# Attention output with queries on partitions from chunk 8 on, its transpose made by the DMA crossbar, and q loaded in token order

## The chip, the cores and the metric

One core of one Trainium2 chip. The metric is the time of one execution on the device, in microseconds (us), lower is better. Before: 225.88 us, median of 3 runs (223.73 to 227.31). Every later run stands beside runs of the kernel before on the same chip, since its medians differed between the chips used, from 224.75 to 226.15 us. Runs more than 1.5% above the fastest of the same kernel are marked slow and left out of the ratios.

## The reference, cut to what matters

```python
# q, k, v: [4 batches, 8 heads, 768 tokens, 64], float32; lam: one decay per head
# attention with exponential decay, block by block (64 tokens each in the reference)
intra = (qb @ kb.T) * Dmask          # Dmask[i, j] = lam ** (i - j) for j <= i, else 0
out   = intra @ vb + (qb * lam_pow) @ kv_state
kv_state = lam_block * kv_state + (kb * rev_pow).T @ vb
x = out.transpose(0, 2, 1, 3).reshape(3072, 512)
h = x @ w_in                          # [3072, 2048]
g = where(h >= 1, h, where(h <= -1, 0, (h + 1) ** 2 / 4))
return g @ w_out                      # [3072, 512], float32
```

## The kernel before

It works in 24 chunks of 128 tokens; four chunks make a stage of 512 tokens for the two dense layers. All loads of q, k and v, all crossbar transposes and all stores of the output are issued by SyncE (SP), one after the other. A scheduler in the kernel, run while it is built, decides the order on each engine: every operation is added with an engine, an estimate, its prerequisites and a due time.

The path of a chunk: load k, q, v in float32; GpSimd (POOL) scales k and q by powers of the decay into bf16 (`ks`, `qs`); SP issues the crossbar transposes of both (`kT`, `qT`, from chunk 6 on; before that TensorE transposes); TensorE forms scores (`ps`, `pt`); VectorE masks them (`sc`); TensorE forms the output (`po`), and ScalarE copies it as x^T (`xT`) into the operand of the first layer.

```python
def f_kx(c):                                   # one crossbar transpose of k for each chunk
    kT[c] = qtp.tile([128, HP, 128], BF16, name="kT", tag="kT")
    nc.sync.dma_start_transpose(out=kT[c], in_=ks[c].rearrange("p h d -> p (h d)"))

def f_qx(m, e):                                # and two of q for each pair of chunks
    nc.sync.dma_start_transpose(out=qT_tile(m)[:, e], in_=qs[m, e].rearrange("p h d -> p (h d)"))
# ...
def f_o(c):                                    # output: features on partitions, tokens as columns
    for hp in range(HP):
        if cb > 0:
            nc.tensor.matmul(po[:, hp], lhsT=ubd[(c - 1) % NUB][:, hp, :], rhs=q_cols(c, hp),
                             start=True, stop=False)
        for hi in range(2):                    # v is padded with zeros to 128 columns
            nc.tensor.matmul(po[:, hp], lhsT=vi[c % NV][:, hp, hi].rearrange("p a d -> p (a d)"),
                             rhs=sc_sb[c][:, hi, hp, :], start=(cb == 0 and hi == 0), stop=(hi == 1))
# ...
def f_load(c, x, wait):                        # q: a pair of chunks in one load, 512 B pieces
    if x == 0:
        t = lq.tile([128, H, 2, D], F32, name="x0f", tag="x0f")
        i = q[b, :, s0:s0 + 2 * C, :].rearrange("h (j e) d -> j h (e d)", e=2)
        d = nc.sync.dma_start(out=t.rearrange("p h e d -> p h (e d)"), in_=i)
```

## Time and profile before

| | before |
|---|---|
| median | 225.88 us |
| profiled run | span 224.4 us, clock 0.999, fast |
| TensorE busy | 206.8 us (92%) |
| from chunk 8's k load to the last q or k transpose | 51.2 to 155.0 us: 103.8 us, 87 issues on SP |

The last row is a count of mine: in the trace of SP, from the issue of the load of chunk 8's k to the issue of the last transpose of q or k. I call it the queue's stretch and use it for every kernel below. In the views, PE is TensorE, PEld its weight loads, DVE VectorE, ACT ScalarE, POOL GpSimd and SPq the issuing by SP; L362 is line 362 of that kernel's file; `ph`, `py` and `pu` hold results of the first layer, the second layer and the state.

The prediction shows the busy table and the slices. Two more views of the kernel before are needed to compare. The first is the chain of work that ended last, as shares of the span; the second is TensorE's one wait for the landing of a transfer (us in total, times, longest):

```profile
PE 62%; DMA 17%; SPq 5%; POOL 5%; issue 3%; ACT 3%; DVE 3%; POOLq 0%; ACTq 0%
```

```profile
PE ps L314 <- DMA kT<-ks: 0.6, 1, 0.6
```

TensorE waits 0.6 us for a transpose in the whole run. And this is what SP does (start us, length us, line, operation):

```profile
84.28 0.58 SPq L460 DMA_DIRECT2D x0f<-in_q_dram  x1
85.37 1.20 SPq L286 DMA_TRANSPOSE kT<-ks  x1
86.64 0.56 SPq L464 DMA_DIRECT2D x1f<-in_k_dram  x1
87.30 0.52 SPq L464 DMA_DIRECT2D x2f<-in_v_dram  x1
87.87 1.18 SPq L464 DMA_DIRECT2D x1f<-in_k_dram  x1
89.16 3.06 SPq L289 DMA_TRANSPOSE qT<-qs  x2
```

Add a start and its length, and the next start follows within 0.05 to 0.5 us. The lengths in the whole stretch sum to 98.1 of its 103.8 us: SP issues almost without a pause, though the prediction counted only 70 us of shortest issue times (0.58 us a load, 1.2 a transpose, 0.37 a store). So 28 us are issues that took longer than their shortest, as the 3.06 us for two transposes above; what SP spends them on, the profile doesn't show. In the transposes it is not waiting for data: counted chunk by chunk, each transpose of k or q in the stretch was issued 2.7 to 9.6 us after GpSimd had written its source. I had these rows before I predicted, and did not sum them.

### The profile page before, as it was taken

The page shows a single profiled execution, that of the slowest core. Times are in us where ns is not written, and L with a number is a line of the kernel's source. Part 1 is how long each engine was busy: PE and PEld are TensorE (multiplying, and loading weights), DVE is VectorE, ACT ScalarE, POOL GpSimd, SP SyncE. Part 2 cuts the span into 40 slices and gives each one's busy share as a digit, 9 for nine tenths or more (in the row PEclk, how much of TensorE's full clock was granted, in tenths as well). Part 3 has the DMA queues.
Part 4 walks back from the last instruction along what each step waited for, and adds up shares of the span by engine and source line. Part 5 has one row for each costly group of instructions (what it writes and reads, how often), then busy time and mean ns, then how long its engine had stood idle before and what let it go on. Part 6 is the DMA issues. An engine that isn't in the chain of part 4 may idle for free.

```text
span 224.4 us, 4691 instructions
## 1 busy us (share of the span) xinstructions
PE 206.8 (92%) x1904; PEld 136.4 (61%) x1904; DVE 144.0 (64%) x218; ACT 123.5 (55%) x221; POOL 64.8 (29%) x65
## 2 busy tenths in 40 slices
PE   0497997999998999999989999999999999999993
PEld 0385544768577877777666766677767744444442
DVE  2678198879949786779387439976656554554301
ACT  3455767547547676666467456676655445445120
POOL 7471084026716360916151028521000000000000
PEclk9999999999999999999999999999999999999999
DMA  5999999999799999989999899986111001110212
GB/s 132 244 192 201 196 243 199 175 208 243 106 232 196 188 207 192 168 211 126 221 151 316 220 197 252 232 159 152 47 47 50 15 31 50 47 47 0 93 50 95
DMA packets 89974, 34.40 MB, mean 153 GB/s; under 512 B 70368, under 2 KB 87008, under 8 KB 89952
## 3 DMA queue, kind: packets, MB, share of 16 engines
q1 hardware_dynamic: 85584, 29.89, 67.2%
q0 software_dynamic: 4224, 4.19, 11.9%
q8 instruction: 15, 0.25, 0.5%
q14 instruction: 7, 0.06, 0.1%
q10 hardware_dynamic: 144, 0.00, 0.0%
HBM read 27.27 MB, written 6.29 MB: 150 GB/s over the span
## 4 chain that ended last, share of the span: by engine, by line
PE 62%; DMA 17%; SPq 5%; POOL 5%; issue 3%; ACT 3%; DVE 3%; POOLq 0%; ACTq 0%
PE py L405 25%; PE ph L362 25%; DMA x0f<-in_q_dram 8%; DMA x2f<-in_v_dram 5%; DMA x1f<-in_k_dram 4%; PE po L334 3%; POOL ks L242 3%; SPq L286 3%; POOL qs L246 2%; PE ps L314 2%; SPq L464 1%; ACT r L370 1%; PE po L331 1%; PE pu L295 1%; PE py L399 1%
## 5 line engine op out<-in xcount | busy, mean ns | idle before, releaser
L362 PE MATMUL ph<-xT,w_in_sb 128*128 128x128 bf16 (+2 forms) x880 | 94.0, 255 | 1.4 <-ACT r L370 1.4
L370 ACT ACTIVATE r<-ph,one 128x512 bf16<-128x512 f32 (+2 forms) x96 | 64.6, 679 | 52.5 <-PE ph L362 34.2
L405 PE MATMUL py<-w_out_sb,gT 128*128 128x512 bf16 x368 | 92.1, 379 | 0.0
L362 PEld LDWEIGHTS <-w_in_sb 128*128 128x128 bf16 x880 | 65.4, 98 | 24.9 <-issue 2.8
L378 DVE TENSOR_SCALAR t<-r 128x1024 bf16<-128x1024 bf16 x48 | 27.3, 570 | 40.3 <-ACT r L370 40.3
L405 PEld LDWEIGHTS <-gT 128*128 128x128 bf16 x368 | 33.9, 98 | 31.4 <-DVE gT L386 0.2
L386 DVE TENSOR_TENSOR gT<-w,t 128x1024 bf16<-128x1024 bf16 x48 | 41.2, 858 | 1.7
L246 POOL TENSOR_TENSOR qs<-x0f,tab_q 128x512 bf16<-128x512 f32 x24 | 29.5, 1250 | 37.1 <-DMA x0f<-in_q_dram 21.9
L381 DVE TENSOR_TENSOR w<-r,t 128x1024 bf16<-128x1024 bf16 x48 | 37.3, 777 | 1.3
L242 POOL TENSOR_TENSOR ks<-x1f,tab_k 128x512 bf16<-128x512 f32 x20 | 25.4, 1275 | 37.4 <-DMA x1f<-in_k_dram 17.5
L324 DVE TENSOR_TENSOR sc<-ps,causal 128x512 bf16<-128x512 f32 x20 | 13.8, 690 | 13.6 <-PE pt L314 13.4
L410 ACT COPY osb<-py 128x512 f32<-128x512 f32 x23 | 13.5, 587 | 12.0 <-PE py L405 10.1
L341 ACT CAST xT<-po 128x512 bf16<-128x512 f32 x24 | 14.1, 587 | 10.7 <-PE po L334 5.5
L334 PE MATMUL po<-sc,vi 128*128 128x128 bf16 x192 | 18.9, 224 | 0.6 <-DVE sc L322 0.5
L260 ACT CAST vi<-x2f 128x512 bf16<-128x512 f32 x24 | 14.8, 618 | 7.8 <-DMA x2f<-in_v_dram 7.8
L299 ACT CAST ubd<-pu 64x256 bf16<-64x256 f32 x40 | 14.6, 365 | 5.2 <-PE pu L295 4.9
L334 PEld LDWEIGHTS <-vi 128*128 128x128 bf16 x192 | 15.0, 101 | 3.2 <-issue 1.3
L331 PE MATMUL po<-qT,ubd 128*128 128x128 bf16 x80 | 14.8, 221 | 0.2 <-ACT xT L341 0.2
L324 DVE TENSOR_TENSOR sc<-pt,causal 128x512 bf16<-128x512 f32 x20 | 13.6, 680 | 0.0
L265 PE MATMUL pt<-ident,ks 128*128 128x128 bf16 x24 | 2.8, 249 | 8.2 <-DVE ks L242 8.0
L331 PEld LDWEIGHTS <-ubd 128*128 128x128 bf16 x80 | 7.9, 99 | 1.6
L295 PE MATMUL pu<-vi,ks 128*128 128x128 bf16 x80 | 8.2, 228 | 0.3
(55 smaller groups left out, 88.2 us busy)
## 6 DMA issues: line engine op xcount, KB each, us to landing
x1f<-in_k_dram SPq DMA_DIRECT2D x24, 256.0 KB, 5.3
x0f<-in_q_dram SPq DMA_DIRECT2D x12, 512.0 KB, 5.5
x2f<-in_v_dram SPq DMA_DIRECT2D x24, 256.0 KB, 5.4
out_dram<-osb SPq DMA_DIRECT2D x23, 256.0 KB, 2.7
w_in_sb<-in_moe_w_in_dram POOLq DMA_DIRECT2D x4, 512.0 KB, 8.7
w_out_sb<-in_moe_w_out_dram POOLq DMA_DIRECT2D x4, 512.0 KB, 8.7
qT<-qs SPq DMA_TRANSPOSE x18, 4.4
kT<-ks SPq DMA_TRANSPOSE x18, 3.5
```

Of the source, the lines that this page charges most:

```text
L242: eng.tensor_tensor(ks[c], qkv_ld[c, 1], _bc(tab_k[:, c % NCB, :], 2, D), op=AX.mult)
L246: eng.tensor_tensor(qs[m, e], qkv_ld[m, 0][:, :, e], _bc(tab_q[:, e, m % (NCB // 2), :], 2, D), op=AX.mult)
L260: nc.scalar.copy(out=v_out(vi[c % NV]), in_=qkv_ld[c, 2].rearrange("p (a b) d -> p a b d", b=2))
L324: nc.vector.tensor_tensor(sc_sb[c][:, g], pst[c, g], _bc(causal, 1, HP), op=AX.mult)
L331: nc.tensor.matmul(po[:, hp], lhsT=ubd[(c - 1) % NUB][:, hp, :], rhs=q_cols(c, hp), start=True, stop=False)
L334: nc.tensor.matmul(po[:, hp], lhsT=vi[c % NV][:, hp, hi].rearrange("p a d -> p (a d)"), rhs=sc_sb[c][:, hi, hp, :], start=(cb == 0 and hi ...
L362: nc.tensor.matmul(ph[:, j * m:(j + 1) * m], lhsT=w_in_sb[:, ko, (ni + j) * 128:(ni + j + 1) * 128], rhs=xT[s][:, ko, part * m:(part + 1) ...
L370: nc.scalar.activation(out=r_t[grp][:, i, cs], in_=ph_t[s, ni, part][:, cs], func=AF.Relu, bias=one[:, 0:1])
L378: nc.vector.tensor_scalar(t_t[grp], r, 0.5, 1.0, op0=AX.mult, op1=AX.min)
L381: nc.vector.tensor_tensor(w_t[grp], r, t_t[grp], op=AX.subtract)
L386: nc.vector.tensor_tensor(gT[s][:, f - RW * n:f, part * m:(part + 1) * m], w_t[grp].rearrange("p a (b m) -> p (a b) m", m=m), t_t[grp].rea ...
L405: nc.tensor.matmul(py_t[s, ms], lhsT=gT[s][:, ko, ms * 128:(ms + 1) * 128], rhs=w_out_sb[:, ko, :], start=(ko == 0), stop=(ko == FO - 1))
```

## The change

The intent: half of the columns of v that the output's products load are zeros. With the masked scores as weights and v streaming, a head needs 64 columns in place of 128. The output then has queries on partitions, so x must be transposed before the first layer; that is one crossbar transpose for a chunk, off TensorE. Now q is the weight operand of the state's product; it is no longer read in the interleaved order of a pair of chunks but loaded in token order, one load for each chunk in 256 B pieces. The scheduler is told to want the outputs 6 us earlier. Chunks 0 to 7 stay as they are.

```diff
+    DX, DLEAD = 8, 6000
 def f_o(c):
+        if c >= DX:
+            for hp in range(HP if cb > 0 else 0):
+                nc.tensor.matmul(po[:, hp], lhsT=q_cols(c, hp), rhs=ubd[(c - 1) % NUB][:, hp, :],
+                                 start=(hp == 0), stop=True, skip_group_check=True)
+            for h in range(H):
+                nc.tensor.matmul(po[:, h // 2, HD[h % 2]], lhsT=sc_sb[c][:, h % 2, h // 2, :], rhs=vn[c][:, h, :],
+                                 start=(cb == 0 and h == 0), stop=True, skip_group_check=True)
+            return
 def f_x(c):
+        if c >= DX:
+            x_sb[c] = xsp.tile([128, d_model], BF16, name="xs", tag="xs")
+            nc.scalar.copy(out=x_sb[c], in_=pot[c].rearrange("p a b -> p (a b)"))
+            return
+    def f_xx(c):
+        nc.sync.dma_start_transpose(out=xT[sx][:, :, off:off + C], in_=x_sb[c])
 def f_load(c, x, wait):
+        if x == 0 and c >= DX:
+            if c % 2 == 0:
+                qkv_ld[c // 2, 0] = lq.tile([128, 2, H, D], F32, name="x0f", tag="x0f")
+            d = nc.sync.dma_start(out=qkv_ld[c // 2, 0][:, c % 2], in_=q[b, :, s0:s0 + C, :].rearrange("h p d -> p h d"))
-        od, cb = o_due(c), c % NCB
+        od, cb = o_due(c) - (DLEAD if c >= DX else 0), c % NCB
+        if c >= DX:
+            add(("x", c), "SP", 1200, lambda c=c: f_xx(c), [("xs", c)], due=-3, dma=640)
# ... cut: tables and mask for token order, contiguous copy of v, prerequisites, order of the first loads
```

More of the change, by code (lines that the diff above doesn't have):

```diff
@@ L76 @@
     xp = ctx.enter_context(tc.tile_pool(name="xp", bufs=3))
+    xsp = ctx.enter_context(tc.tile_pool(name="xsp", bufs=2))
+    vnp = ctx.enter_context(tc.tile_pool(name="vnp", bufs=4))
     gp = ctx.enter_context(tc.tile_pool(name="gp", bufs=2))
@@ L134, with late_setup @@
         nc.vector.memset(t, 0.0)
+    tab_qn = const.tile([128, NCB, H], F32)
+    causal_n = const.tile([128, 128], F32)
+    def late_setup():
+        nc.scalar.activation(out=tab_qn, in_=arg[:, 0], func=AF.Exp)
+        nc.gpsimd.memset(causal_n, 1.0)
+        nc.gpsimd.affine_select(out=causal_n, in_=causal_n, compare_op=AX.is_ge, fill=0.0,
+                                base=0, pattern=[[1, 128]], channel_multiplier=-1)
     def v_out(t):
@@ L245, in cast_q @@
         qs[m, e] = qkp.tile([128, H, D], BF16, name="qs", tag="qs")
+        if 2 * m >= DX:
+            eng.tensor_tensor(qs[m, e], qkv_ld[m, 0][:, e], _bc(tab_qn[:, (2 * m + e) % NCB, :], 2, D), op=AX.mult)
+            return
         eng.tensor_tensor(qs[m, e], qkv_ld[m, 0][:, :, e], _bc(tab_q[:, e, m % (NCB // 2), :], 2, D), op=AX.mult)
@@ L255, in q_cols @@
         i = c % 2
+        if c >= DX:
+            return qT[c // 2][rows, i, hp, :]
         x = qT[c // 2][rows, 0, hp, i * 64:(i + 1) * 64]
         return bass.AP(x.tensor, x.offset, [list(x.ap)[0], [HP * 128, 2], [1, 64]])
+    vn, x_sb = {}, {}
     def cast_v(c):
+        if c == CPS:
+            late_setup()
+        if c >= DX:
+            vn[c] = vnp.tile([128, H, D], BF16, name="vn", tag="vn")
+            nc.scalar.copy(out=vn[c], in_=qkv_ld[c, 2])
+            return
         nc.scalar.copy(out=v_out(vi[c % NV]), in_=qkv_ld[c, 2].rearrange("p (a b) d -> p a b d", b=2))
@@ L294, in f_u @@
         for hp in range(HP):
-            nc.tensor.matmul(pu[0][:, hp, :], lhsT=pair(ks[c], hp), rhs=v_pair(vi[c % NV], hp),
+            nc.tensor.matmul(pu[0][:, hp, :], lhsT=pair(ks[c], hp), rhs=v_pair(vi[c % NV], hp) if c < DX else pair(vn[c], hp),
                              start=(c % NCB == 0 and hp == 0), stop=True, skip_group_check=True)
@@ L323, in f_m @@
         else:
-            nc.vector.tensor_tensor(sc_sb[c][:, g], pst[c, g], _bc(causal, 1, HP), op=AX.mult)
+            nc.vector.tensor_tensor(sc_sb[c][:, g], pst[c, g], _bc(causal if c < DX else causal_n, 1, HP), op=AX.mult)
     def f_o(c):
@@ L328, in f_o @@
         po = pot[c] = pp_o.tile([128, HP, 128], F32, name="po", tag="po")
+        if c >= DX:
[5 more added lines that the diff above has]
+                                 start=(cb == 0 and h == 0), stop=True, skip_group_check=True)
+            return
         for hp in range(HP):
@@ L340, in f_x @@
             xT[sx] = xp.tile([128, KO, MS], BF16, name="xT", tag="xT")
+        if c >= DX:
+            x_sb[c] = xsp.tile([128, d_model], BF16, name="xs", tag="xs")
+            nc.scalar.copy(out=x_sb[c], in_=pot[c].rearrange("p a b -> p (a b)"))
+            return
         nc.scalar.copy(out=xT[sx][:, :, off:off + C].rearrange("p h (j e) -> p h j e", e=2),
                        in_=pot[c].rearrange("p h (e j) -> p h j e", e=2))
+    def f_xx(c):
+        sx, off = c // CPS, (c % CPS) * C
+        nc.sync.dma_start_transpose(out=xT[sx][:, :, off:off + C], in_=x_sb[c])
     gT, r_t, t_t, w_t, py_t, ph_t, osb = {}, {}, {}, {}, {}, {}, {}
@@ L456, in f_load @@
         b, s0 = c // NCB, (c % NCB) * C
-        if x == 0:
+        if x == 0 and c >= DX:
+            if c % 2 == 0:
+                qkv_ld[c // 2, 0] = lq.tile([128, 2, H, D], F32, name="x0f", tag="x0f")
+            d = nc.sync.dma_start(out=qkv_ld[c // 2, 0][:, c % 2], in_=q[b, :, s0:s0 + C, :].rearrange("h p d -> p h d"))
+        elif x == 0:
             t = lq.tile([128, H, 2, D], F32, name="x0f", tag="x0f")
@@ L482 @@
             need = [("w",) + w_seen[-1], ("cast", CPS - 1, 1) if len(w_seen) > 1 else None] if w_seen else \
-                [("cast", CPS - 2, 2), ("cast", CPS - 2, 1)]
+                [("cq", CPS // 2 - 1, 1)]
             if gated is not None:
@@ L493 @@
         gated = len(w_seen) - 2 if last_c is not None and w_seen and not isinstance(order[order.index(it) - 1], int) else None
-        for x in (1, 2) if it % 2 else (1, 0, 2) if it == 0 else (0, 1, 2):
+        for x in (1, 0, 2) if it == 0 or it >= DX else (1, 2) if it % 2 else (0, 1, 2):
             need = [("w",) + w_seen[-2] if w_seen else None]
-            if x == 0:
+            if x == 0 and it >= DX:
+                add(("ld", it, 0), "SP", 590, lambda i=it: f_load(i, 0, None),
+                    [("cq", it // 2 - LQ, 0), ("cq", it // 2 - LQ, 1)] + need, due=pos_ * 1e-3, dma=1190)
+            elif x == 0:
                 add(("lq", it // 2), "SP", 700, lambda i=it, wait=gated: f_load(i, 0, wait),
@@ L516 @@
             add(("cq", m, i), "POOL", 1060, lambda m=m, i=i: cast_q(m, i, nc.gpsimd),
-                [("lq", m), ("cq", m, 0) if i else None, old, ("qT",) + old[1:]])
+                [("lq", m) if c < DX else ("ld", c + i, 0), ("cq", m, 0) if i else None, old, ("qT",) + old[1:]])
             if m < XQ:
@@ L542 @@
             add(("s", c, 0), "PE", mm(*[128] * 4) + 190, lambda c=c: f_s2(c),
-                [("kT", c) if c < XT else ("t", c), ("qT", m, 0), ("qT", m, 1), ("m", c - 1, 0), ("m", c - 1, 1)], due=od - 2500, extra=FILL)
+                [("kT", c) if c < XT else ("t", c), ("qT", m, 0) if c < DX or c % 2 == 0 else None, ("qT", m, 1) if c < DX or c % 2 else None, ("m", c - 1, 0), ("m", c - 1, 1)], due=od - 2500, extra=FILL)
         for h in range(2):
@@ L548 @@
             add(("m", c, h), "DVE", 690, lambda c=c, h=h: f_m(c, h), [("s", c, h if c < CPS else 0), ("o", c - 3), ("m", c, 0) if h else None])
-        add(("o", c), "PE", mm(*[128] * (12 if cb else 8)), lambda c=c: f_o(c),
+        add(("o", c), "PE", mm(*[128] * (12 if cb else 8)) if c < DX else mm(*[128] * (4 if cb else 0)) + 8 * 33, lambda c=c: f_o(c),
             [("m", c, 1), ("cast", c, 2), ("ub", c - 1, 0) if cb else None, ("ub", c - 1, 1) if cb else None,
-             ("x", c - 1), ("o", c - 1)], due=od, extra=FILL)
-        add(("x", c), "ACT", 600, lambda c=c: f_x(c), [("o", c), ("x", c - 1), ("l1", (c // CPS - 2) * FO - 1)])
+             ("x", c - 1) if c <= DX else ("xs", c - 1), ("o", c - 1)], due=od, extra=FILL)
+        add(("x", c) if c < DX else ("xs", c), "ACT", 600, lambda c=c: f_x(c),
+            [("o", c), ("x", c - 1), ("xs", c - 1), ("x", c - 2), ("l1", (c // CPS - 2) * FO - 1)])
+        if c >= DX:
+            add(("x", c), "SP", 1200, lambda c=c: f_xx(c), [("xs", c)], due=-3, dma=640)
     n1, last = 0, None
```

## The prediction

> **What bounds the kernel now.** I read the busy table and the slices of the page first, then the groups of instructions, then the sums by stretch of time, the chain of waits, and last the order of TensorE and of the DMA queue instruction by instruction.
>
> ```profile
> PE 206.8 (92%) x1904; PEld 136.4 (61%) x1904; DVE 144.0 (64%) x218; ACT 123.5 (55%) x221; POOL 64.8 (29%) x65
> ...
> PE   0497997999998999999989999999999999999993
> ...
> DMA  5999999999799999989999899986111001110212
> ...
> q1 hardware_dynamic: 85584, 29.89, 67.2%
> ```
>
> TensorE is busy 92% and its empty slices are the first few and the last. "Busy" flatters a pipelined engine, so I laid the start times of successive matmuls against the spacing of an undisturbed stream (56 ns for 128 columns, 216 ns for 512). From 40 us to the end only some 6 us are lost, 2.3 us of them in three waits, at 69.7, 113.0 and 133.6 us; about 11 us are lost between 8 and 40 us, and the first matmul starts at 7.9 us. So from 40 us on a microsecond taken out of TensorE's stream comes off the end, if nothing else takes its place.
>
> The second row matters as much: the DMA engines are as full as TensorE until about 155 us, then nearly empty. All loads of q, k and v, all crossbar transposes and all stores are issued by one queue, SP. By stretch (start:end, length, busy time of PE, PEld, DVE, ACT, POOL, clock, DMA share, GB/s):
>
> ```profile
> 89.50:92.50 3.00, 3.00 (x37) 2.19 (x35) 2.93 (x4) 2.35 (x4) 2.90 (x3) 1.00 1.37 217
> ...
> 104.00:107.00 3.00, 3.00 (x46) 2.32 (x44) 2.96 (x5) 2.06 (x5) 0.75 (x1) 1.00 0.63 129
> ...
> 180.00:200.00 20.00, 20.00 (x94) 9.11 (x93) 10.87 (x18) 9.37 (x15) 0.00 (x0) 1.00 0.07 27
> 40.00:150.00 110.00, 108.18 (x1214) 78.15 (x1213) 82.78 (x115) 67.03 (x121) 44.18 (x35) 1.00 1.09 200
> ```
>
> The first is load traffic, the second a row of transposes alone, which leaves the engines half empty; from 40 to 150 us the mean share is 1.09 (two packets may be in flight on one engine), and after 180 us it is 0.07. The chain of waits between 60 and 113 us is not TensorE but a loop of SP, DMA and POOL:
>
> ```profile
> 66.73 1.19 SPq L286
> 67.97 3.64 DMA x1f<-in_k_dram
> 71.78 1.57 POOL ks L242
> 73.34 1.01 SPq L286
> 74.40 4.44 DMA x0f<-in_q_dram
> ```
>
> A load lands, POOL scales it, SP issues its transpose, and the next load stands behind it in the same queue. Here two paths run side by side, nearly equally long.
>
> **What the Trainium skill says.** "TensorE: Matmul & The Clock Gate", section Back-to-back issue gap, gives about 60 cycles for 1 to 64 columns against 134 for 128, with a floor near 25 ns, or near 62 ns if the sequencer decodes matmuls. The second floor cannot hold here: matmuls of 128 columns start every 56 ns, and the row-split score pairs make two in 57 ns. No stream of 64 columns is in this trace. Its section LDWEIGHTS says that loading takes columns / 1.2 ns whatever the contraction; weights stay 128 columns in this change, so a load could become the bound. The trace shows loads of 98 ns that overlap streams of 56 ns, and that decides nothing below 56. "DMA: Bandwidth & Descriptors", section Specifications, wants 512 B or more per transfer for line rate. The trace agrees: phases of pure 256 B packets move some 850 packets per us, phases of 512 B some 575, so 256 KB in 256 B pieces take 1.2 us and 512 KB in 512 B pieces 1.8 us. "Perfetto Trace Analysis", section What "DMA-bound" means, names a second bound, the issuing sequencer. The trace has it: a transpose keeps SP 1.2 us at least.
>
> ```profile
> L289 SPq DMA_TRANSPOSE qT<-qs x18: 1202/1381/2939, 53.4 to 152.3; - x18
> ...
> DMA to landing us min/median/max: 2.5/4.4/6.0
> ```
>
> **The change part by part.** It touches chunks 8 to 23, sixteen of 24.
>
> TensorE, removed: in the output each chunk has 4 matmuls of the state and 8 of the scores, all of 128 columns; half of v's padded weights are zeros. Now scores are weights and v streams 64 columns. A chunk looked like this:
>
> ```profile
> 121.69 0.22 PE L331 MATMUL po<-qT,ubd 128*128 128x128 bf16 x1
> 121.74 0.28 PE L334 MATMUL po<-sc,vi 128*128 128x128 bf16 x2
> 121.86 0.22 PE L331 MATMUL po<-qT,ubd 128*128 128x128 bf16 x1
> ```
>
> From 121.69 to 121.86 are three matmuls, 56 ns each; twelve take 0.68 us. The kernel's own scheduler prices a 64-column one at 33 ns. It prices 128 columns at 56 and the switch to row-split matmuls at 190 ns, both of which agree with the trace, so I take 33 as an estimate. Saving: 16 x 8 x (56.3 - 33) ns = 3.0 us; 3.5 us at the best (64/2.4 + 2.6 = 29 ns), nothing if the weight load holds the pace at 56.
>
> TensorE, moved: the order of instructions puts the first piece of the first layer (four matmuls of 384 columns, 0.65 us) ahead of the third chunk's output, into a gap of 0.66 us at 20.8 us where TensorE waits for the mask. Worth 0.5 us if the weights have landed. The rest of the head is the same.
>
> ScalarE, VectorE, POOL: counts and shapes stay. Output copy (587 ns), v cast (618 ns), mask (690 ns) and the scaling of q (1,250 ns) keep their sizes and become contiguous; I give nothing for it.
>
> DMA, added: (a) 16 transposes of x, 128 KB each; at 512 packets of 256 B and 850 per us, 0.6 us of the engines and 1.2 us of SP each. (b) q of the sixteen chunks by 16 loads of 256 B pieces for 8 of 512 B: 16 x 1.2 - 8 x 1.8 = +4.8 us of the engines, and 8 more issues of 0.6 us. Over the stretch from the load of chunk 8's k to the last q or k transpose the queue goes from 32 single loads, 7 pair loads, 36 transposes, 12 stores to 48, 0, 50, 14. With 1.2, 1.8, 0.6 and 0.75 us the engines' work goes from 82 to 98 us; SP's issue time (0.58, 1.2 and 0.37 us) from 70 to 93 us. Before, that stretch lasts from 51 to 155 us, 104 us.
>
> Also new: x reaches the first layer by copy, SP's turn and landing (some 5 us) rather than by the copy alone. The scheduler asks for outputs 6 us earlier, which covers it; but the inputs are then needed earlier too.
>
> **Does the DMA still fit?** Laying TensorE's new order out at measured spacings, chunk 23's scores come at about 172 us, so its last transpose must be issued by about 168: 117 us after 51. The 98 us of engine work and the 93 us of issue fit apart. Before, though, 82 us took 104, because waits, SP-bound transposes and loads don't overlap wholly. At that ratio 98 us take 125, and the last transpose is 8 us late; if the added transposes fill holes of the engines, nothing is late. The tightest places are chunks 17 to 23, where ScalarE's cast of v stands in line ahead of a ReLU that TensorE waits for. My estimate is 2 us of new waits: the schedule leaves margin, and the old queue idled some 6 us in that stretch.
>
> Sum: 225.9 - 3.0 - 0.5 + 2.2 = 224.6 us.
>
> **Rivals.** First, *TensorE's saving arrives whole*: attention has run up to 17 us ahead of need (chunks 15 to 17 in the old trace), so added traffic eats only that lead: 222.0 to 222.5 us. For it: DMA is idle after 157 us, and stores can move there. Against it: at chunks 8 and 20 the old lead is zero. Second, *the queue becomes the bound*: an x transpose at the head of SP waits for TensorE's output and holds up loads behind it, so lateness feeds itself; TensorE then stalls 6 to 9 us between 110 and 175 us: 229 to 232 us. For it: the loop in the chain and the 104 us for 82. Third, *64 columns cost as much as 128* because the 128-column weight load paces them: no saving, and whatever the queue costs: 225.5 to 229 us. Against it is only the scheduler's 33 ns and the pairs at 28 ns, which load 64-row weights.
>
> **Range and chances.** A full saving and no wait gives 222; faster by over 2% needs under 221.4, for which I see no source: 0.06. Slower by over 2% is above 230.4, the second rival nearly whole: 0.16. The rest, 0.78, is within 2%. Range 221.6 to 231.0, wider above.
>
> **What would show it.** The eight score matmuls: start every 33 ns (29 to 40 right, 56 wrong). TensorE's losses after 100 us: under 1 us more is the first rival, over 5 the second. DMA must stay full until about 165 to 172 us instead of 155, with transposes of x landing in 3 to 5 us; the last 45 us should be as before, as there is only dense matmul. SP's waits should show the x transpose waiting for ScalarE. If the time falls under 221, the old waits at 113 and 133.6 us, or the head, have gone too, which I do not count on; if it exceeds 231, the queue's order is worse than its work.

## The result, and the profile after

| | before | after |
|---|---|---|
| median, range | 225.64 us, 223.73 to 227.31 (4 runs) | 232.18 us, 231.44 to 234.35 (4 runs) |
| ratio, 95% interval | | 1.0335, 1.0228 to 1.0442: slower |
| the queue's stretch | 103.8 us, 87 issues | 124.7 us, 112 issues |
| TensorE's stops over 0.24 us, 40 to 100 / 100 to 185 us | 0.7 / 1.6 us | 8.7 / 6.4 us |

A ratio here is the mean time of one kernel's fast runs over that of the other's fast runs of the same rounds, so not quite the ratio of the medians. A stop is what the start-to-start distance of two matmuls has over the spacing of an undisturbed stream; 30 of 1,904 matmul records are missing from the trace after, which can make a stop look longer.

The prediction was 224.6 us and its range ended at 231.0. The time is outside. The busy rows of the page after:

```profile
PE 202.1 (88%) x1874; PEld 132.1 (57%) x1904; DVE 149.4 (65%) x218; ACT 122.8 (53%) x222; POOL 62.2 (27%) x67
...
PE   0588989988999787989979998988899999999994
...
DMA  5999999999899797989989999978996221100212
...
q1 hardware_dynamic: 102608, 31.99, 73.4%
...
PE 48%; DMA 35%; SPq 6%; POOL 6%; issue 2%; ACT 1%; DVE 0%; POOLq 0%; ACTq 0%
```

TensorE has sevens and eights in slices between 75 and 104 us where it had nines, the DMA row stays full three slices longer (to about 173 us in place of 151), and the last row, the chain, has DMA at 35% where it had 17%. From 40 to 150 us (start:end, length, busy time of PE, PEld, DVE, ACT, POOL with counts, clock, DMA share, GB/s):

```profile
40.00:150.00 110.00, 99.26 (x1132) 71.33 (x1150) 78.41 (x106) 63.16 (x115) 36.63 (x31) 1.00 1.09 191
```

The DMA share from 40 to 150 us is 1.09 as before, while the bytes fall from 200 to 191 GB/s. Full engines are not what changed: as much is in flight, and less arrives. What TensorE waits for, and what SP waits for (us in total, times, longest):

```profile
PE ps L338 <- DMA qT<-qs: 5.5, 6, 1.5
PE ph L402 <- DMA xT<-xs: 4.3, 5, 1.5
```

```profile
SPq L467 <- ACT osb L450: 35.2, 7, 9.1
SPq L383 <- ACT r L410: 13.4, 11, 2.5
```

Eleven stops of TensorE for a landing, of q as often as of x. SP's list puts 13.4 us on transposes of x that wait for ScalarE, behind a ReLU of the dense layer (L410). That row needs care. In the instructions themselves, SP starts each of the 14 transposes of x within the stretch 0.1 us after the issue before it, once 0.5, as it does any other; only the last two, after the stretch, have real gaps ahead (1.7 and 3.2 us). And ScalarE had written each of the 14 between 0.7 and 4.6 us before SP's turn came. The list names what came last by its own inference; the order of the tiles is the surer guide. The wait for stores (L467), which SP has after the stretch, was 57.0 us before. For k and q it is the same: written in time, then standing in the queue. Chunk 10's k was scaled at 70.68 to 71.83 us and its transpose issued at 80.77:

```profile
70.68 1.15 POOL L253 TENSOR_TENSOR ks<-x1f,tab_k 128x512 bf16<-128x512 f32 x1 [4.70 <-PE ph L402]
```

```profile
80.77 2.12 SPq L310 DMA_TRANSPOSE kT<-ks  x1
```

Over the stretch each transpose of k or q was issued 1.8 to 10.9 us after its source had been written. The queue at the same place as above, and the chain there:

```profile
84.25 1.23 SPq L500 DMA_DIRECT2D x0f<-in_q_dram  x1
85.59 1.20 SPq L310 DMA_TRANSPOSE kT<-ks  x1
87.30 1.20 SPq L383 DMA_TRANSPOSE xT<-xs  x1
88.61 1.20 SPq L313 DMA_TRANSPOSE qT<-qs  x1
```

```profile
87.30 2.63 DMA xT<-xs
89.97 1.96 PE ph L402 x32
91.93 0.22 PE po L355 x4
92.16 0.23 PE po L358 x8
```

The first layer starts at 89.97 us when the transposed x has landed. The same lines show what the change was made for: 8 products of 64 columns take 0.23 us, 29 ns each, where four products of the state with 128 columns take 0.22.

In the stretch the lengths of SP's issues now sum to 117.6 of 124.7 us, against 93 us of shortest times; the part beyond the shortest, 25 us, is no more than before (28).

So TensorE got what was promised, the head too (its stops before 40 us fall from 10.8 to 9.6 us), and some 11 us of new stops came: measured -3.5 (16 chunks x 8 x (56.3 - 28.8) ns) - 1.2 + 11.2 = +6.5 us, where 11.2 is what is left of the measured difference. Summing all the lost spacing after 40 us, with the 30 missing records taken off at 0.2 us each, gives 17.2 against 5.9 us, 11.3 more: the same.

### The profile page after: what moved, and what is told of

Its sections match the earlier page's. It is cut to its first block, busy times and chain, and to the rows that moved or that the text cites. A ratio compares the mean times of both kernels' runs of the same rounds, so it can differ in the third digit from the quotient of the medians.

```text
span 230.3 us, 4712 instructions
## 1 busy us (share of the span) xinstructions
PE 202.1 (88%) x1874; PEld 132.1 (57%) x1904; DVE 149.4 (65%) x218; ACT 122.8 (53%) x222; POOL 62.2 (27%) x67
## 4 chain that ended last, share of the span: by engine, by line
PE 48%; DMA 35%; SPq 6%; POOL 6%; issue 2%; ACT 1%; DVE 0%; POOLq 0%; ACTq 0%
PE py L445 21%; PE ph L402 21%; DMA xT<-xs 10%; DMA w_out_sb<-in_moe_w_out_dram 7%; DMA x0f<-in_q_dram 7%; DMA w_in_sb<-in_moe_w_in_dram 5%; DMA qT<-qs 5%; SPq L508 3%; DMA x1f<-in_k_dram 2%; POOL qs L260 2%; PE ps L338 2%; POOL qs L258 2%; POOL ks L253 1%; PE py L439 1%; POOL w_in_sb L166 1%
## 5 line engine op out<-in xcount | busy, mean ns | idle before, releaser
L410 ACT ACTIVATE r<-ph,one 128x512 bf16<-128x512 f32 (+2 forms) x96 | 64.6, 678 | 56.6 <-PE ph L402 37.7
L258 POOL TENSOR_TENSOR qs<-x0f,tab_qn 128x512 bf16<-128x512 f32 x16 | 18.8, 1173 | 16.9 <-DMA x0f<-in_q_dram 15.3
L450 ACT COPY osb<-py 128x512 f32<-128x512 f32 x23 | 13.5, 585 | 15.2 <-PE py L445 13.8
L348 DVE TENSOR_TENSOR sc<-ps,causal_n 128x512 bf16<-128x512 f32 x16 | 11.1, 691 | 15.8 <-PE pt L338 15.8
L260 POOL TENSOR_TENSOR qs<-x0f,tab_q 128x512 bf16<-128x512 f32 x8 | 9.4, 1198 | 14.4 <-DMA x0f<-in_q_dram 14.3
L338 PE MATMUL ps<-qT,kT 64*128 64x128 bf16 x80 | 7.8, 217 | 5.7 <-DMA qT<-qs 5.5
L338 PEld LDWEIGHTS <-kT 64*128 64x128 bf16 x160 | 4.9, 94 | 10.6 <-issue 6.8
L348 DVE TENSOR_TENSOR sc<-pt,causal_n 128x512 bf16<-128x512 f32 x16 | 10.9, 681 | 0.0
L375 ACT CAST xs<-po 128x512 bf16<-128x512 f32 x16 | 9.3, 579 | 2.2 <-PE po L358 2.0
L282 ACT CAST vn<-x2f 128x512 bf16<-128x512 f32 x16 | 9.8, 615 | 0.1
L284 ACT CAST vi<-x2f 128x512 bf16<-128x512 f32 x8 | 5.0, 619 | 9.2 <-DMA x2f<-in_v_dram 9.1
L319 PEld LDWEIGHTS <-ks 128*128 128x128 bf16 x80 | 6.0, 102 | 4.7 <-POOL ks L253 2.4
```

The source lines that it names most:

```text
L258: eng.tensor_tensor(qs[m, e], qkv_ld[m, 0][:, e], _bc(tab_qn[:, (2 * m + e) % NCB, :], 2, D), op=AX.mult)
L260: eng.tensor_tensor(qs[m, e], qkv_ld[m, 0][:, :, e], _bc(tab_q[:, e, m % (NCB // 2), :], 2, D), op=AX.mult)
L338: nc.tensor.matmul(pst[c, hi][:, hp, :], lhsT=kT[c][HD[hi], hp, :], rhs=q_cols(c, hp, HD[hi]), start=True, stop=True)
L348: nc.vector.tensor_tensor(sc_sb[c][:, g], pst[c, g], _bc(causal if c < DX else causal_n, 1, HP), op=AX.mult)
L410: nc.scalar.activation(out=r_t[grp][:, i, cs], in_=ph_t[s, ni, part][:, cs], func=AF.Relu, bias=one[:, 0:1])
```

## The experiments

Theories. *Issue*: SP issues in order and has no free time, so every added instruction lengthens its stretch; transposes come late and TensorE stops. *Engine work*: the added bytes and packets fill the 16 engines. *Coupling*: only the transpose of x, which waits for TensorE and ScalarE, holds the queue up. *Lead*: the 6 us of earlier due times make TensorE reach chunk 8's work before its inputs.

**1. Parts of the change.** Three kernels: the change with q loaded in pairs again (its rows are then in the wrong order, so the result is wrong on purpose); the kernel before with q in token order, and of the rest only the order of the loads and the mask that go with it; the change with x transposed by TensorE in place of the crossbar.

```diff
# a_pairq, on the kernel after
-            d = nc.sync.dma_start(out=qkv_ld[c // 2, 0][:, c % 2], in_=q[b, :, s0:s0 + C, :]...)
+            i = q[b, :, s0:s0 + 2 * C, :].rearrange("h (j e) d -> j h (e d)", e=2)      # 512 B pieces, 8 loads
# b_tokq, on the kernel before: q loads, scaling, mask and q's columns as in the change; v and output as before
+            nc.scalar.copy(out=xT[sx][:, :, off:off + C], in_=pot[c])
# c_xpe, on the kernel after (DLEAD 2500)
-        nc.sync.dma_start_transpose(out=xT[sx][:, :, off:off + C], in_=x_sb[c])
+            nc.tensor.transpose(out=xpt[c][:, hp, :], in_=x_sb[c][:, hp * 128:(hp + 1) * 128], identity=ident)
+        nc.vector.tensor_copy(xT[sx][:, :, off:off + C], xpt[c])
```

> The changed kernel, but q of chunks 8 to 23 loaded by pairs of chunks again, 512 B pieces (8 loads instead of 16); the rows of q then stand in the wrong order, so the result is wrong on purpose, and all else is as in the changed kernel. Theory A (the sum of work on the load queue and the DMA engines costs the time, whoever adds it): 4.8 us of engine work and 8 issues go, so the time falls from 232 to about 227 to 229 us. Theory B (only the transposes of x cost: they stand at the head of the queue, wait for TensorE and ScalarE, hold loads up, and x reaches the first layer late): 230.5 to 232 us.

> The kernel before, with one part of the change alone: q of chunks 8 to 23 in token order (16 loads of 256 B pieces), outputs still d on partitions, no transposes of x. A: 225.6 plus a third of the loss, 227 to 229 us. B: 225 to 226.5 us.

> The changed kernel with x transposed by TensorE (4 transposes and a VectorE copy a chunk) and not by the crossbar; q in token order stays. It gives TensorE back 16 x 4 x 56 ns = 3.6 us, about what 64 columns save, and takes 16 transposes from the queue. A: as b_tokq, 227 to 229 us. B: 225 to 226.5 us, the same as before the change.

Measured: a_pairq 230.11 us, ratio 1.024 [1.019, 1.029], stretch 125.6 us. b_tokq 228.73 us, its fast runs 227.21 to 229.32, ratio 1.021 [1.013, 1.028], stretch 107.4. c_xpe 228.88 us, ratio 1.019 [1.013, 1.024], stretch 108.7. So the 16 transposes of x are worth 16 us of stretch, and taking them out brings the time half the way back, although TensorE gets 64 transposes of its own; the lead was shorter there too, which this run does not separate. The q loads alone cost about 2%. Both parts cost, so x's coupling is not the whole of it. The pair loads are a miss for the issue theory: fewer issues, no shorter stretch, though 2 us less time.

**2. Work that waits for nothing.** The kernel before with 16 transposes whose result nobody reads, of data that is there anyway:

```diff
# d_dummyx
+    def f_dx(c):
+        t = dxp.tile([128, HP, 128], BF16, name="dx", tag="dx")
+        nc.sync.dma_start_transpose(out=t, in_=ks[c].rearrange("p h d -> p (h d)"))
+            if c >= 8:
+                add(("dx", c), "SP", 1200, lambda c=c: f_dx(c), [("t", c)], due=-1, dma=640)
# ... cut: GpSimd's later scalings of k wait until the dummy has read its buffer
```

> The kernel before plus 16 crossbar transposes of the scaled k of chunks 8 to 23 into a scratch tile that nobody reads: the load on the queue (1.2 us of issue and 0.6 us of engines each) without the wait for TensorE and without the longer way of x. A: 229 to 232 us. B: 225.5 to 227 us.

Measured: 234.96 us, ratio 1.045 [1.038, 1.052], stretch 127.8. Such a transpose waits for no product and no copy of x, and yet it costs as much as the whole change. Coupling falls as the main cause. A caution: the clock was 0.983 to 0.985 in all runs of this kernel, which at 1.5% makes some 3.5 of the 10 us. The profiled run has a stop of TensorE of 4.5 us at 124 to 129 us, and two slices of lower clock at its end (from 128 to 135 us matmuls of 512 columns start every 427 ns, then every 216 again):

```profile
PEclk9999999999999999999999589999999999999999
```

So a part of what this dummy costs comes through the clock, after the stop.

**3. Issue or engine work?** Three more dummies in the kernel before, chosen so that the two part: 16 loads of 256 KB (much engine work, short issue), 16 copies of 128 KB within the on-chip memory in 1 KB pieces (little engine work, short issue), and 8 transposes of 1,024 columns (the bytes of d_dummyx in half the instructions).

```diff
# f_dummyld
+        nc.sync.dma_start(out=t, in_=k[b, :, s0:s0 + C, :].rearrange("h p d -> p h d"))
# h_dummycp
+        nc.sync.dma_start(out=t, in_=ks[c].rearrange("p h d -> p (h d)"))
# g_dummyx8, for every second chunk
+        nc.sync.dma_start_transpose(out=t, in_=w_out_sb[:, 0:2, :].rearrange("p a d -> p (a d)"))
```

> The kernel before plus 16 plain loads of k (256 KB each, 256 B pieces) into a scratch tile that nobody reads, at the places where d_dummyx had its transposes: 0.6 us of issue and 1.2 us of engines each, the mirror of a transpose (1.2 and 0.6). Theory I: half of what d_dummyx lost, 229 to 231 us. Theory E: twice, 240 us or more. Both bounds at once, added one after the other: as d_dummyx, 233 to 237 us.

> The kernel before plus 16 plain copies of the scaled k within SBUF (128 KB, 1 KB pieces), the same bytes as d_dummyx without the crossbar. If it is the crossbar instruction that is dear (its 1.2 us of issue and 256 B pieces): 225.5 to 228 us. If any further item in this queue costs as much: 233 us or more.

> The kernel before plus 8 crossbar transposes of twice the size (1,024 columns at once) into a scratch tile: the same bytes as d_dummyx in half the instructions. If the issue has a fixed part, an instruction takes well under 2.4 us and the time is 228 to 232 us; if it goes with size alone, 2.4 us each and 233 to 236 us as d_dummyx.

The dummies in their traces (count, shortest/median/longest issue in ns, first and last start), in the order d, f, h, g:

```profile
L291 SPq DMA_TRANSPOSE dx<-ks x16: 1196/1261/2139, 68.1 to 180.2; - x16
```

```profile
L292 SPq DMA_DIRECT2D dx<-in_k_dram x16: 557/573/582, 68.8 to 169.9; - x16
```

```profile
L291 SPq DMA_DIRECT2D dx<-ks x16: 570/582/1532, 68.3 to 169.3; - x16
```

```profile
L291 SPq DMA_TRANSPOSE dx<-w_out_sb x8: 1296/1300/2252, 75.5 to 171.1; - x8
```

A dummy transpose of 1,024 columns keeps SP 1.30 us and one of 512 columns 1.26 (medians): in these dummies the issue is paid for the instruction, not for the size. Experiment 5 limits this. In the table, "issue" is the number of dummies within the stretch times the median, "engines" an estimate from the prediction's 1.2 us for 256 KB and 0.6 us for 128 KB in 256 B packets (for the copies, a quarter of the packets, I put 0.45 us).

| dummies | time, ratio | issue | engines | stretch more than 103.8 |
|---|---|---|---|---|
| d: 16 transposes, 512 columns | 234.96, 1.045 | 18.9 us | 9 us | 24.0 us |
| f: 16 loads, 256 KB | 229.72, 1.023 | 8.6 us | 18 us | 13.5 us |
| h: 16 copies, 128 KB | 232.50, 1.035 | 8.7 us | 7 us | 12.8 us |
| g: 8 transposes, 1,024 columns | 231.95, 1.032 | 9.1 us | 8 us | 14.9 us |

The traces agree with the order of the estimates: the time of SP's packets (the queue's share of 16 engines times the span, 150.8 us before) grew by 5.4, 16.8, 3.0 and 5.9 us for d, f, h and g in the whole run. f has more than twice the engine work of h and the same stretch; g has d's bytes and 9 us less of stretch. The stretch follows the issue, 1.3 to 1.6 us for each us. Why more than one to one I did not isolate; stores that come due in the longer stretch are one or two of the issues. The times follow less neatly: h costs 2.8 us more than f at an equal stretch, and there the copies hold GpSimd's buffers (12.8 us of waits before `ks`), which the loads don't; its clock was 0.983 to 0.993 too. d's transposes hold these buffers as well (15.1 us), so d's time is not the issue alone; f and g hold nothing, and they lose 2.3 and 3.2%.

**4. Another queue for q.** The Trainium skill's page "Trainium Kernel Development and Optimization", Key Constraints, says that all queues share the 16 engines and that issuing from several only saves issue time. That is the very thing short here, so q's loads went to GpSimd's queue. (Transposes from a second queue I did not try: "DMA: Bandwidth & Descriptors", section Silent corruption, warns that two streams that transpose at the same time can corrupt each other. No run here shows it.)

```diff
# e_poolq, on the kernel after
-            d = nc.sync.dma_start(...q...)
+            d = nc.gpsimd.dma_start(...q...)
-                add(("ld", it, 0), "SP", 590, ...)
+                add(("ld", it, 0), "POOL", 900, ...)
```

> The changed kernel with the 16 loads of q of chunks 8 to 23 issued from POOL's queue and not from SP's; the bytes and pieces are the same. What is left open by the first runs is which half of the queue is the bound. Theory I (SP's issue: one instruction after the other, 1.2 us for a transpose): SP is rid of 16 issues of 0.6 us at least and of their waits, some 10 to 15 us, so the time falls to 224 to 228 us. Theory E (the DMA engines themselves): 231 to 233 us.

Measured: 241.84 us, ratio 1.076 [1.071, 1.081], clock 0.969 to 0.986. The stretch is 111.7 us, 13 less than after, as the issue theory has it, but it begins at 65.3 us in place of 51. GpSimd's line tells why:

```profile
37.51 3.63 POOL L500 DMA_DIRECT2D x0f<-in_q_dram  x4
48.99 1.04 POOL L258 TENSOR_TENSOR qs<-x0f,tab_qn 128x512 bf16<-128x512 f32 x1 [7.85 <-DMA x0f<-in_q_dram]
```

Four loads at once, then a scaling of q that stands 7.85 us for its landing with the scaling of k behind it. The experiment moved the bottleneck to another engine that works in order. As a test it is inconclusive.

**5. The same work in fewer instructions.** If the issue is paid for each instruction, merging two transposes should help where the bytes stay. In the change: k and q of a chunk scaled into one tile and transposed by one instruction. In the kernel before: the two q transposes of a pair in one.

```diff
# j_kq, on the kernel after
+            kq[c] = kqp.tile([128, 2, H, D], BF16, name="kq", tag="kq")       # k in [:, 0], q in [:, 1]; 3 buffers
+            nc.sync.dma_start_transpose(out=kqT[c].rearrange("p a h d -> p (a h) d"), in_=kq[c].rearrange("p a h d -> p (a h d)"))
# i_bq2, on the kernel before
-        nc.sync.dma_start_transpose(out=qT_tile(m)[:, e], in_=qs[m, e].rearrange("p h d -> p (h d)"))
+        nc.sync.dma_start_transpose(out=qT_tile(m).rearrange("p a h d -> p (a h) d"), in_=qs2[m].rearrange("p a h d -> p (a h d)"))
```

> The changed kernel with the transposes of k and q of a chunk made in one crossbar instruction (both scaled into one tile, 1,024 columns; chunks 8 to 23). g_dummyx8 showed 1.30 us of issue for 1,024 columns against 1.26 us for 512, so SP issues 16 instructions and some 20 us less, while the DMA engines move the same bytes in the same pieces. Theory I (SP's issue is the bound): the stretch from chunk 8's k to the last transpose shrinks from 125 to about 103 us, the waits of TensorE go, and the saving of 64 columns arrives: 221 to 224 us. Theory E (the engines' bytes): 230 to 232 us.

> The kernel before with the two q transposes of a pair of chunks in one instruction: 9 issues less, 11 us of SP. Theory I: the queue has room, but TensorE was the bound of this kernel with 2.3 us of waits in all, so at best 223 us, 223 to 225. Theory E: 224 to 226 us, as before.

Measured: j_kq 228.18 us, ratio 1.018 [1.012, 1.023], correct; 16 issues fewer bring the stretch from 124.7 to 108.1 us. i_bq2 223.43 us (222.87 to 225.14), ratio 0.996 [0.991, 1.002], correct; 9 issues fewer, stretch 96.8. In its chain TensorE has nearly all, and waits of TensorE for a transpose come to 0.4 us:

```profile
PE 86%; DMA 5%; DVE 3%; ACT 3%; issue 2%; POOL 0%; SPq 0%; POOLq 0%
```

The bytes and the data packets of both kernels are those of their parents. The engines had room in the change: over its stretch the DMA share was 1.06, over j_kq's 1.18. So engine work is not what made the stretch long. But only 4 of the 6.5 us came back, and the issue theory's 221 to 224 us and stretch of 103 are missed. One reason is to be seen in SP's rows. A merged transpose is not issued in 1.30 us there; the rows of j_kq and of o_kqx2 (the next experiment), where single ones of k and q in the change have medians of 1.22:

```profile
L326 SPq DMA_TRANSPOSE kqT<-kq x16: 1242/1866/3772, 64.1 to 159.9; - x16
```

```profile
L326 SPq DMA_TRANSPOSE kqT<-kq x16: 1248/2269/3370, 64.1 to 155.9; - x16
```

The shortest is 1.24 us, as for a dummy, the median 1.87 and 2.27. By the count used above, SP's lengths beyond the shortest are 29 us in j_kq, 36 in o_kqx2 and 32 in i_bq2, where the change has 25. Whether fuller engines hold SP up there, no run shows.

**6. The lead, and x merged too.** What makes the rest: the earlier due times, or the issues that x still has? One number changed in the kernel after and in j_kq; x transposed for two chunks at once; and both.

```diff
# m_lead3 (on after), n_kqlead3 (on j_kq), o_kqx2lead3 (on o_kqx2)
-    DX, DLEAD = 8, 6000
+    DX, DLEAD = 8, 3000
# o_kqx2, on j_kq (output tiles 7 in place of 8, for space)
+            if c % 2 == 0:
+                x_sb[c // 2] = xsp.tile([128, 2, d_model], BF16, name="xs", tag="xs")
+        nc.sync.dma_start_transpose(out=xT[sx][:, c % CPS - 1:c % CPS + 1].rearrange("p a h m -> p (a h) m"), in_=x_sb[c // 2].rearrange("p a d -> p (a d)"))
```

> The changed kernel with one number changed: the lead of the decay work is 3.0 us in place of 6.0. If the lead makes the waits at 49 to 90 us, the time falls from about 232 to 229 to 230 us and the two gaps of TensorE at 49 and 54.5 us (1.0 and 1.1 us) go. If the queue's issue alone makes them, the stretch from chunk 8's k load to the last q or k transpose stays near 125 us and the time at 231 to 233 us.

> The k and q transposes of a chunk merged in one instruction (228.2 us before, stretch 108 us) and the lead 3.0 us in place of 6.0. Lead theory: 224 to 226 us. Issue theory: 228 us as without the shorter lead, with the stretch near 108 us in both.

> k and q transposes merged, and the x transposes of two chunks merged too, lead 6.0 us as in the changed kernel: some 8 issues of 1.3 us fewer than in the kernel with merged k and q. Issue theory: the stretch falls from 108 to about 98 us and the time from 228.2 to 225 to 227 us. Lead theory: the time stays at 227 to 229 us, whatever the stretch.

> Both: merged k and q, x merged for two chunks, lead 3.0 us. If both causes count, 221 to 224 us, below the kernel before (225) by the 3 us of narrower products that were expected at first. If one of the theories is the whole of it, it equals the better of the two kernels that have one part alone, within 1 us.

(By "the lead of the decay work" the first text means the lead of the attention's outputs, `DLEAD`.) Measured, beside 226.15 us of the kernel before in this call:

| | median | ratio | stretch |
|---|---|---|---|
| m_lead3 | 234.80 us (fast runs 233.07 to 235.76) | 1.035 [1.028, 1.043] | 127.8 us |
| n_kqlead3 | 227.79 us | 1.007 [1.001, 1.014] | 110.7 us |
| o_kqx2 | 225.78 us | 0.998 [0.994, 1.003] | 104.3 us |
| o_kqx2lead3 | 227.28 us | 1.004 [0.998, 1.010] | 105.1 us |

The lead is not the cause: halving it makes the change no faster, and with x merged it is, if anything, worse. With k and q merged alone it may be worth something: n_kqlead3's ratio is 1% lower than j_kq's, though on another chip and with medians within 0.4 us. Merging x brought the change level with the kernel before, inside the 225 to 227 us that the issue theory had; its stretch came to 104.3 us, not to the 98 expected. Yet the 3.5 us of TensorE still don't come out below it.

**7. Two last tries to bring the saving out.** In o_kqx2 GpSimd waits 16.8 us for TensorE to release the three merged tiles, so a fourth; and the new form from chunk 12 on only, with q merged in pairs below it.

```diff
# p_kqx2b4, on o_kqx2
-    kqp = ... bufs=3;  kqtp = ... bufs=3;  NO = 7
+    kqp = ... bufs=4;  kqtp = ... bufs=4;  NO = 5
# q_dx12, on o_kqx2 with the merged q of i_bq2 for chunks 6 to 11
-    DX, DLEAD = 8, 6000;  NO = 7
+    DX, DLEAD = 12, 6000;  NO = 5
```

> The kernel with k, q and x merged, with four buffers of the merged k and q tiles in place of three (and five of the output tiles in place of seven). If the buffers delay the transposes, GpSimd's waits for TensorE (16.8 us) go and the time falls from 225.8 to 223 to 225 us. If the queue's order and issue alone set it, the stretch stays at 103 to 106 us and the time at 225 to 227 us.

> The new form of attention from chunk 12 on in place of 8, with k, q and x merged there, and the q transposes of a pair merged in the chunks below. Half the narrower products (1.7 us of TensorE), 4 single q loads and 2 merged x transposes in place of 8 and 4. If the queue's issue decides, its stretch is about 97 to 100 us and the time 222 to 224 us, as or below the kernel before with merged q (223.4). If the new form itself costs something that isn't in the queue, the time is 224 to 226 us.

Measured: p_kqx2b4 225.51 us (225.45 to 228.07), ratio 1.003 [0.998, 1.008]: the buffers were not it. q_dx12 228.56 us, ratio 1.017 [1.010, 1.024], though its stretch of 100.7 us is short: a miss. At 101.5 us TensorE waits for a transpose and soon after for an output tile, of which I had left five:

```profile
101.54 0.23 PE L365 MATMUL ps<-kqT 64*128 64x128 bf16 x1 [1.47 <-DMA kqT<-kq]
...
105.34 1.50 PE L473 MATMUL py<-w_out_sb,gT 128*128 128x512 bf16 x4 [2.40 <-ACT osb L478]
```

Its clock was 0.984 to 0.992, lower right after these stops, so this kernel tests its buffers as much as its start.

What is left of the waits in o_kqx2, the best of the changed kernels:

```profile
PE ps L357 <- DMA kqT<-kq: 4.2, 4, 1.5
...
PE ph L422 <- DMA xT<-xs: 0.6, 1, 0.6
```

4.8 us of waits for a transpose stand against the kernel before's 0.6. That is about the size of what TensorE saves. With a stretch as long as before (104.3 against 103.8 us), TensorE, now faster, comes to the same transposes sooner and waits for them. This fits the profiles but was not isolated; whether a queue with some 10 us less would let the saving out stays open. So does one thing about all of these runs: the scheduler lays every engine's order out anew for each edit, so each kernel differs from its parent in order as well as in the edit; no run holds the order fixed.

The kernels on one scale, by the stretch of the profiled run (without e_poolq, whose stretch begins late):

| kernel | stretch | ratio |
|---|---|---|
| i_bq2 | 96.8 us | 0.996 |
| q_dx12 (five output tiles, low clock) | 100.7 | 1.017 |
| before | 103.8 | 1 |
| o_kqx2 | 104.3 | 0.998 |
| o_kqx2lead3 | 105.1 | 1.004 |
| b_tokq | 107.4 | 1.021 |
| j_kq | 108.1 | 1.018 |
| c_xpe | 108.7 | 1.019 |
| p_kqx2b4 (profiled: the slowest of its five runs) | 109.7 | 1.003 |
| n_kqlead3 | 110.7 | 1.007 |
| h_dummycp | 116.6 | 1.035 |
| f_dummyld | 117.3 | 1.023 |
| g_dummyx8 | 118.7 | 1.032 |
| after | 124.7 | 1.034 |
| a_pairq | 125.6 | 1.024 |
| m_lead3 | 127.8 | 1.035 |
| d_dummyx | 127.8 | 1.045 |

Up to 105 us, q_dx12 apart, the ratio stays within 0.4% of 1; from 116 us on every kernel is 2.3 to 4.5% slower. Between, the stretch alone does not order them: where the late landings fall may count too. b_tokq's 2% at 3.6 us of added stretch is the weakest fit, and its cause stays open. The fastest of all is the kernel before with merged q; its median is 223.43 us beside 224.82, its ratio 0.4% below 1 with 1 inside the interval.

## Why the prediction was wrong, point by point

- *What bounds the kernel now*: right as far as it went, two paths side by side. It read the second path as a loop in which SP waits for GpSimd's scaling, and weighed it by the work of the DMA engines. The tiles do not show SP waiting: the `ks` that ends at 73.34 us in the chain is chunk 10's, and its transpose was issued at 81.99, while the one issued at 71.44 read a tile written at 65.47. The chain infers who released SP from the last semaphore event that it saw, and that was not the one needed. The engines' share did not move (1.09); SP's issuing, of data long ready, did.
- *The 64-column term*: predicted 33 ns and 3.0 us, measured 29 ns and 3.5 us. Right, sized small; it was named as the best case. The third rival, that the weight load paces them, falls.
- *The head, 0.5 us*: the piece of the first layer did move into the gap at 20.8 us; stops before 40 us fell by 1.2 us.
- *Does the DMA still fit?* This step failed. It compared 98 us of engine work and 93 us of issue, apart, with 117 us of room. It had a better number at hand, 82 us taking 104 and so 98 taking 125, and the stretch measured was 124.7. I set it aside for "2 us of new waits" (2.2 in the sum), on the ground that added transposes might fill holes of the engines and the old queue idled 6 us. The holes of the engines are no use, as SP, not the engines, has no time; and SP's 6 us of idling are the gaps between back-to-back instructions. In place of the 2.2 us stand 11.2.
- *Why 125 was right*: in part by luck. The ratio was formed of engine work; what it describes is issue. The dummies show that a ratio of engine work would have failed for them (f against h).
- *Second rival, the queue becomes the bound, 229 to 232 us*: this is what came, at its upper edge. It said that an x transpose that waits for TensorE holds up the loads behind it. Within the stretch SP has no such gaps and x was always written before SP's turn, and d_dummyx shows that transposes which wait for no product cost as much. Nor are the stops between 110 and 175 us: 8.7 of 15.1 us come before 100, from chunk 8's first work on. "At chunks 8 and 20 the old lead is zero" was the hint. That the tightest places would be chunks 17 to 23 was wrong with it.
- *Signs*: DMA full until about 165 to 172 us (last transpose 175.8), x landing in 3 to 5 us (median 3.8), SP waiting for ScalarE before x: all came, though the wait for ScalarE is in the list of waits and not in SP's spacing. The sign of over 5 us more of TensorE's losses after 100 us was just missed: 6.4 against 1.6 us is 4.8 more. The chances gave 0.16 to slower; with the 125 us taken at its word the sum is 225.9 - 3.5 + 8 = 230.4 us, at the threshold.

## What to carry to other kernels

When one in-order queue issues everything, sum the lengths of its issues in the stretch that matters before adding to it: 98 of 104 us was full, and the shortest issue times (70 us) hid that. Full DMA engines do not say whether the engines or the issuing queue is short; fewer, larger instructions with the same bytes tell them apart, and are the first thing to try, though a merged transpose kept SP up to twice as long here as a single one. A saving on an engine that runs level with another path was worth nothing here while that path stayed as long.

## What the Trainium skill lacked or had wrong

- "Perfetto Trace Analysis", What "DMA-bound" means: for a bound of the engines or of the issuing sequencer it says that large descriptors are what matter. For the sequencer, here, the number of instructions mattered: the packets stayed as they were (256 B in the transposes), 16 instructions fewer took 16.6 us out of the stretch (124.7 to 108.1). The size is not free either: a transpose of 1,024 columns took SP 1.30 us as a dummy and 1.87 for k and q, against 1.26 and 1.22 for 512 (medians).
- "DMA: Bandwidth & Descriptors", DMA Transpose (X-bar): the section gives no issue time, and the cycle counts in the page's part on trn3 B0 are for other shapes. Here a transpose of 128 x 512 bf16 keeps SP 1.19 us at least and 1.2 to 1.5 in the median, a load of 256 KB 0.57, a copy of 128 KB on the chip 0.58.
- "TensorE: Matmul & The Clock Gate", Back-to-back issue gap: its roofline of about 81 ns for streams of weight load and 128 columns (131 for 512) does not hold here: with a weight load for each product the state's products start every 56 ns, those of 64 columns with 128-column weights every 29 ns (0.23 us for 8), and those of 512 columns every 216 ns; all are close to its isolated formula (64/2.4 + 2.5 = 29 ns).
- "TensorE: Matmul & The Clock Gate", Why this matters for your kernels: "No PE-idle gaps >~3µs between matmul bursts". A stop of 4.5 us in d_dummyx agrees (a slice at half clock at its end, mean 0.983). A stop of 3.3 us at 149 us in g_dummyx8 was followed by no lower clock. But a stop of 2.0 us at 70 us in j_kq, and two of 1.6 and 2.6 us within 4 us in q_dx12, were each followed by two slices at 0.8 (means 0.990 and 0.992), while a_pairq stayed at 1.0 with single stops of up to 2.1 us. So gaps below the page's limit were followed by a lower clock in two runs, and one just above it was not; what decides it no run here shows.
